# Pooled-query attention with a feed-forward block: the low parts of q and k by an accumulating DMA, and row maxima in units of 512 keys

## The chip, the cores and the metric

One core of one Trainium2 chip. The metric is the device time of one execution in microseconds, from the first to the last instruction and what the launch adds around it; several runs are taken and their median is used. The profile is of one execution.

## The reference

Attention over 8 batches x 8 heads, 1152 keys and head dimension 64, where each two neighbouring queries are averaged first, so there are 576 queries. Then a feed-forward block on the 4608 tokens.

```python
q_pool = q.reshape(B, H, S // 2, 2, D).mean(axis=3)
scores = scale * np.matmul(q_pool, k.transpose(0, 1, 3, 2))
scores = scores - np.max(scores, axis=-1, keepdims=True)
attn = np.exp(scores); attn = attn / (attn.sum(-1, keepdims=True) + 1e-9)
x = np.matmul(attn, v)            # -> (4608, 512)
h = x @ w_in                      # (512, 2048)
return (h - np.tanh(h)) @ w_out   # (2048, 512)
```

All is float32. The kernel gets that precision on TensorE from two reduced-precision (fp32r) parts: `hi`, the rounded value, and `lo`, value minus `hi`; a product is hi·hi + hi·lo + lo·hi.

## The kernel before

Two heads of a batch are a *pair*: 32 pairs, with head 0 in partitions 0 to 63 and head 1 in 64 to 127. For a pair, `raw` (128 x 1728 floats) holds the summed queries (576) and the keys (1152); `w.hi` (`kq_h` in the profile) and `w.lo` (`kq_l`) are its two parts.

Every engine's instructions are issued in the order in which the program names them (`InOrder`), so a place in the program is a place in that engine's queue. DMAs go through SyncE's queue (`sp`).

Each pair has two phases, and each has 18 places (`NS = 18`):

- the *scores phase*, places 0 to 17. Each place makes one tile of scores, 128 keys x 288 queries for both heads, with four pairs of matmuls (hi·hi, lo·hi, hi·lo, and a row that subtracts the maximum: `sel` x `m_row`). ScalarE takes the exponential into `p`; GpSimd adds three `p` at a time into `sum`.
- the *PV phase*, places 18 to 35: 72 matmuls `ps<-p,v` into two outputs that ScalarE copies to `o_s` (after places 26 and 35), then `sums` (24 matmuls `sum,ones`, copied to `s_s`).

All PSUM results of the attention stage, scores, maxima, outputs and sums alike, take turns in one ring of four buffers (`ring`, tile `ps`, 2 x 512 floats each).

The exponential needs each query's maximum beforehand. It is taken from hi·hi of the *next* pair during the scores phase of the current one: `max_part(pi, i)` multiplies 128 queries by 384 keys for both heads, and VectorE reduces 128 x 768 to 128 x 2 (`mx<-ps`). Four query tiles x three thirds of the keys make units 0 to 11, at places 1, 2, 4, 5, 7, 8, ... 16, 17. The last 64 queries of both heads form one tile (`q_last`) and two units (12, 13) that are done at the end of the pair before. `max_row` (place 17) reduces the parts to `nm`, transposes them (`tr`) and sends them through DRAM (`m_dram`) to `m_row`.

What else is put at places of pair `p` (NS = 18):

- NS: `query_sums` (VectorE, `raw<-q`) and `high` (ScalarE, `kq_h<-raw`, `q_last<-raw`) for pair p+2
- NS + 8: `low` for pair p+1, the subtraction on VectorE (`kq_l<-raw,kq_h`), after `o_s` of the first half
- NS + 12: `load` of raw and q for pair p+3; place 2: `load_v` for p+1
- the weights of the feed-forward block, in 16 blocks of six steps. A step is taken at places NS + 3, 6, 11 and 15 of pairs from 2 on, so the steps repeat over three pairs. First step: ScalarE's absolute value (`w_t<-w_raw`) and VectorE's `w_hl<-w_off`; second: three VectorE operations on `w_t`; third: `w_hl<-w_raw,w_t` and the next block's loads; fourth: `w_t<-w_hl`; fifth: `w_hl<-w_hl,w_t` and the stores to `wi_dram` or `wo_dram`; sixth: nothing. `w_hl` is one buffer, so the next block's first VectorE operation on it waits for that store.
- in the last four pairs, the first chunk of x for the feed-forward block (VectorE `x_r`, `x_l`; ScalarE `x_h`).

The feed-forward stage then runs over 9 chunks of 512 tokens x 16 blocks of hidden units.

Of the kernel before, what the change touches and what calls it, by code (L numbers as in the profile page):

```python
# [7 lines left out]
F32 = mybir.dt.float32  # L8
F32R = mybir.dt.float32r
I32 = mybir.dt.int32  # L10
U16 = mybir.dt.uint16
AF = mybir.ActivationFunctionType
ALU = mybir.AluOpType
AX = mybir.AxisListType
# [32 lines left out]
def attention_ffn_kernel(  # L47
# [16 lines left out]
    P = 128  # L64
    B, NP, _, _, SQ = q.shape
    S = k.shape[-1]
    D = P // 2
    KT = S // P
    KQ = SQ + S
    HQ = SQ // 2  # L70
    CH = S // 3
# [5 lines left out]
    pe, act, dve, pool, sp = (InOrder(tc, e) for e in (nc.tensor, nc.scalar, nc.vector, nc.gpsimd, nc.sync))  # L77
# [32 lines left out]
    class X:  # L110
# [25 lines left out]
        def high(self, c):  # L136
            act.activation(self.h[:, c], self.r[c], AF.Copy)

        def low(self, eng, c):
            eng.tensor_tensor(self.l[:, c], self.r[c], self.h[:, c].bitcast(F32), op=ALU.subtract)  # L140
# [14 lines left out]
    with ExitStack() as actx:  # L155
        new = lambda name, bufs, **kw: actx.enter_context(tc.tile_pool(name=name, bufs=bufs, **kw))
        st = new("st", 1)
        hip, lop = new("hi", 2), new("lo", 1)
        vp = new("vp", 2)
        ppool = new("pp", 2)  # L160
        sp_pool = new("sums", 1)
        op = new("op", 2)
# [17 lines left out]
        def rows(t, h):  # L180
            return t[h * D:h * D + D]

        def psum():
            return ring.tile([P, 2, 512], F32, name="ps")
# [10 lines left out]
        pairs = {}  # L195
# [15 lines left out]
        def high(pi, parts=1):  # L211
# [4 lines left out]
            for h in range(2):  # L216
                act.activation(rows(q_last[pi % 2], h)[:, h * D:h * D + D], rows(w.raw, h)[:, 4 * P:SQ], AF.Copy)

        def low(pi):
            w = pairs[pi]  # L220
            w.lo = lop.tile([P, KQ], F32R, name="kq_l")
            dve.tensor_tensor(w.lo, w.raw, w.hi.bitcast(F32), op=ALU.subtract)

        def load_v(pi):
            w = pairs[pi]
# [1 line left out]
            sp.dma_start(w.v, v[w.b, w.hp])  # L227


        order = [(t, c) for t in range(4) for c in range(3)] + [(4, 0), (4, 2)]  # L230

        def max_part(pi, i):

            w = pairs[pi]
            t, c = order[i]
            q0 = t * P
            ps = psum()
            if t < 4:
                for h in range(2):
                    pe.matmul(ps[:, h, 0:CH], rows(w.hi, h)[:, q0:q0 + P], rows(w.hi, h)[:, SQ + c * CH:SQ + (c + 1) * CH],  # L240
                              start=True, stop=True)
                dve.tensor_reduce(w.mx[:, t, c], ps[:, :, 0:CH], axis=AX.X, op=ALU.max)
            else:
                n = min(2, 3 - c)
                for a in range(n):
                    pe.matmul(ps[:, a, 0:CH], q_last[pi % 2], w.hi[:, SQ + (c + a) * CH:SQ + (c + a + 1) * CH],
                              start=True, stop=True)
                dve.tensor_reduce(w.mx[:, 4, c // 2, 0:n], ps[:, 0:n, 0:CH], axis=AX.X, op=ALU.max)
# [70 lines left out]
        class W:  # L319
# [17 lines left out]
            def steps(self, then):  # L337
# [23 lines left out]
                def low():  # L361
# [6 lines left out]
                    high,  # L368
                    lambda: ts(self.t, self.hl[:, 0], -0x800000, None, op0=ALU.bitwise_and),
                    low,  # L370
                    lambda: None,
                ]
# [21 lines left out]
        NS = 2 * KT  # L394

        def add(pi, place, f, *args):
            at.setdefault((pi, place), []).append(lambda: f(*args))

        for pi in range(1, n_pair):
            for i in range(12):  # L400
                add(pi - 1, i // 2 * 3 + 1 + i % 2, max_part, pi, i)
            if pi >= 2:
                for i in range(12, 14):
                    add(pi - 2, 2 * NS, max_part, pi, i)
            add(pi - 1, NS - 1, max_row, pi)
        for pi in range(n_pair):
            if pi >= 2:
                add(max(pi - 3, 0), NS + 12 if pi > 2 else 0, load, pi)
                add(pi - 2, NS, query_sums, pi)
                add(pi - 2, NS, high, pi)  # L410
            if pi >= 1:
                add(pi - 1, 2, load_v, pi)
                add(pi - 1, NS + 8, low, pi)
            if pi % NP == NP - 1 and pi < n_pair - 1:
                add(pi + 1, 10, fetch_sums, pi // NP)
                add(pi + 1, NS + 10, reciprocals, pi // NP)
# [26 lines left out]
        load_v(0)  # L443
        query_sums(0)
        high(0, 2)
        for i in range(9):
            max_part(0, i)
        max_row(0, 0, 3)
        low(0)
        for i in range(9, 14):  # L450
            max_part(0, i)
        max_row(0, 3, 4)
        query_sums(1)
        high(1)
        for i in range(12, 14):
            max_part(1, i)
        blocks[0].load()

# [4 lines left out]
        for pi in range(n_pair):  # L463
            w = pairs[pi]
            ps = [Half(), Half()]
# [101 lines left out]
    for ci in range(len(chunks)):  # L567
        c = Chunk()
# [8 lines left out]
        for f in range(NF):  # L577
            n = ci * NF + f
# [71 lines left out]
```

## Time and profile before

| | |
|---|---|
| median of 3 runs | 1634.74 us (1633.24 to 1636.42) |
| the profiled execution | 1633.7 us, its span 1631.9 us, granted clock 0.996 |
| busy: PE, VectorE, ScalarE, GpSimd | 97%, 78%, 58%, 68% |
| attention stage | scores of pair 0 at 26.75 us, PV of pair 31 at 813.86 us |
| subtraction `kq_l` | 32 x 2783 ns = 89.1 us of VectorE |
| exponentials | 576 x 653 ns on ScalarE |
| reductions `mx` 128 x 768 | 416 x 953 ns on VectorE |

How to read it: DVE is VectorE, ACT ScalarE, POOL GpSimd, SP SyncE, PEld TensorE's weight loads, and a q behind a name is that engine's queue. A row of the groups gives out<-in, the shape, the count, then busy us and the mean ns of one, then the idle time just before them and what ended it. A row in order of time gives start and length in us; in brackets is the idle time before it and its releaser. Several like instructions in a row are merged with their count. A matmul's time includes its way through the array, so successive ones overlap, and a PE that is 97% busy isn't at its peak: a step between starts (0.13 us for two 288-column matmuls on the two halves of the array) tells the rate.

### The profile page before, as it was taken

The numbers are of one execution on the slowest core, as the hardware profiler recorded it, in microseconds if no ns is written. First come the engines' busy times: TensorE is split into PE (matmuls) and PEld (weight loads), VectorE is DVE, ScalarE is ACT, GpSimd is POOL, SyncE is SP. The second block draws the span as 40 slices with busy tenths as digits, with TensorE's granted clock in tenths as the row PEclk, the third lists the DMA queues.
The fourth block names the chain that finished last, engine by engine and source line by source line (L and its number), as shares of the span: only waits on it lengthen the run. The fifth ranks groups of instructions, "written<-read, shape, count | busy, mean of one in ns | idle before, by whom it ended". The sixth has DMA issues, their size and how long they took to land.

```text
span 1631.9 us, 30673 instructions
## 1 busy us (share of the span) xinstructions
PE 1586.2 (97%) x12012; PEld 1228.4 (75%) x12012; DVE 1280.5 (78%) x1621; ACT 938.5 (58%) x1584; POOL 1113.3 (68%) x749
## 2 busy tenths in 40 slices
PE   5999999999999999999999999999999999999998
PEld 4777676776776776777768888888888888888886
DVE  6788888898889898969447777777777777777776
ACT  3565565565655656656535656555555656555554
POOL 3777786776767767778756666666757675666654
PEclk9999999999999999999999999999999999999999
DMA  4335444344453554333471101001010101020000
GB/s 169 107 119 197 167 150 182 133 183 162 155 214 135 200 182 160 131 123 100 152 310 34 65 7 48 31 7 65 13 65 14 65 14 65 13 65 10 30 1 26
DMA packets 79602, 166.15 MB, mean 102 GB/s; under 512 B 11874, under 2 KB 38498, under 8 KB 77410
## 3 DMA queue, kind: packets, MB, share of 16 engines
q1 hardware_dynamic: 79458, 164.20, 28.3%
q8 instruction: 94, 1.54, 0.4%
q14 instruction: 50, 0.41, 0.1%
HBM read 126.12 MB, written 38.04 MB: 101 GB/s over the span
## 4 chain that ended last, share of the span: by engine, by line
PE 83%; DVE 11%; DMA 2%; issue 2%; ACT 2%; POOL 0%; SPq 0%; POOLq 0%; DVEq 0%; ACTq 0%
PE ps L37 35%; PE ps_h L37 24%; PE ps_o L37 24%; DVE mx L37 3%; DVE w_t L37 3%; DVE kq_l L37 1%; DVE w_hl L37 1%; DMA wi_dram<-w_hl 1%; DVE raw L37 1%; ACT w_t L37 1%; DMA m_dram<-tr 0%; SPq L37 0%; DMA q<-in_q_dram 0%; ACT q_last L37 0%; POOL sum L37 0%
## 5 line engine op out<-in xcount | busy, mean ns | idle before, releaser
L37 DVE TENSOR_REDUCE mx<-ps 128x2 f32<-128x768 f32 x448 | 396.6, 924 | 86.9 <-PE ps L37 85.0
L37 POOL TENSOR_TENSOR sum<-p,p 128x576 f32<-128x576 f32 x192 | 300.6, 1566 | 196.7 <-ACT p L37 196.5
L37 ACT ACTIVATE p<-ps 128x576 f32<-128x576 f32 x576 | 353.2, 653 | 112.1 <-PE ps L37 93.7
L37 POOL TENSOR_SCALAR g_m<-g_u 128x512 uint8<-128x512 f32 (+1 forms) x145 | 250.6, 1728 | 197.6 <-ACT g_u L37 182.5
L37 POOL TENSOR_TENSOR sum<-sum,p 128x576 f32<-128x576 f32 x192 | 301.1, 1568 | 29.2 <-ACT p L37 15.1
L37 PE MATMUL ps<-kq_h 64*128 64x288 f32 (+1 forms) x1920 | 289.3, 345 | 28.0 <-DVE mx L37 17.6
L37 PE MATMUL ps<-p,v 128*64 128x288 f32 x2304 | 286.4, 407 | 0.1
L37 DVE SCALAR_TENSOR_TENSOR ps_w<-g_u,ps_h 128x512 f32<-128x512 f32 (+1 forms) x145 | 100.4, 693 | 191.3 <-ACT g_t L37 191.2
L37 PEld LDWEIGHTS ps<-p,v 128*64 128x64 f32 x2304 | 162.6, 137 | 114.4 <-ACT p L37 6.9
L37 POOL TENSOR_TENSOR g_lo<-g_s,g_hi 128x512 fp32r<-128x512 f32 (+1 forms) x145 | 186.6, 1287 | 89.5 <-ACT g_hi L37 89.5
L37 PE MATMUL ps_o<-w,g_hi 128*128 128x512 f32 x792 | 244.5, 390 | 1.0 <-ACT g_hi L37 1.0
L37 PEld LDWEIGHTS ps<-kq_h 64*128 64x128 f32 x1920 | 181.3, 187 | 80.8 <-DVE mx L37 33.0
L37 ACT ACTIVATE g_u<-ps_h 128x512 f32<-128x512 f32 (+1 forms) x145 | 85.8, 591 | 244.0 <-PE ps_h L37 242.3
L37 PE MATMUL ps_h<-x_h,w 128*128 128x512 f32 (+1 forms) x800 | 214.8, 390 | 0.0
L37 ACT ACTIVATE g_s<-g_u,pc 128x512 f32<-128x512 f32 x290 | 193.2, 714 | 11.3
L37 PEld LDWEIGHTS ps_h<-x_h,w 128*128 128x128 f32 x800 | 149.6, 188 | 32.4
L37 PEld LDWEIGHTS ps_o<-w,g_hi 128*128 128x128 f32 x792 | 148.5, 188 | 33.6 <-ACT g_hi L37 1.4
L37 PE MATMUL ps<-kq_l,kq_h 64*128 64x288 f32 x1152 | 171.8, 295 | 0.0
L37 PE MATMUL ps<-kq_h,kq_l 64*128 64x288 f32 x1152 | 171.5, 294 | 0.0
L37 PE MATMUL ps<-m_row,sel 64*128 64x288 f32 x1152 | 171.2, 293 | 0.0
L37 PE MATMUL ps_o<-w,g_lo 128*128 128x512 f32 x396 | 154.8, 391 | 0.6 <-POOL g_lo L37 0.5
L37 DVE COPY_PREDICATED g_s<-g_m,g_t 128x512 f32<-128x512 uint8 (+1 forms) x145 | 108.4, 748 | 15.0
(92 smaller groups left out, 2368.3 us busy)
## 6 DMA issues: line engine op xcount, KB each, us to landing
raw<-in_k_dram SPq DMA_DIRECT2D x32, 576.0 KB
q<-in_q_dram SPq DMA_DIRECT2D x32, 576.0 KB
v<-in_v_dram SPq DMA_DIRECT2D x32, 576.0 KB
x_dram<-o_s SPq DMA_DIRECT2D x32, 288.0 KB
x_l<-x_dram SPq DMA_DIRECT2D x9, 1024.0 KB
out_dram<-o_f SPq DMA_DIRECT2D x36, 256.0 KB
w_raw<-in_w_in_dram SPq DMA_DIRECT2D x8, 1024.0 KB
w_off<-in_w_in_dram SPq DMA_DIRECT2D x8, 1024.0 KB
```

Source lines behind the costliest of these rows:

```text
L37: i = f(*args, **kwargs)
```

## The change

1. `low` no longer subtracts on VectorE, except for pair 0. Instead ScalarE writes -raw, rounded to fp32r like `hi`, into the tile of `lo` (`minus_high`, place NS + 9 of the pair two before), and GpSimd issues a DMA that adds `raw` onto it (`low`, place NS + 16 of the pair two before). `lo` has two buffers instead of one.
2. The maxima of the four full query tiles (4 x 1152 keys) are taken in nine units of 512 keys instead of twelve of 384. A unit that crosses from one query tile to the next is in two pieces, each with its own matmuls and reduction: units 2, 4 and 6 (128 + 384, 256 + 256, 384 + 128). There are still three parts for each tile, 24 matmuls and 12 reductions. The units stand at places 1, 3, 5, ... 17.
3. In the prologue, seven units, then pair 0's subtraction, then the last two; and `minus_high` and `low` for pair 1 ahead of its two `q_last` units.

```diff
-        hip, lop = new("hi", 2), new("lo", 1)
+        hip, lop = new("hi", 2), new("lo", 2)
...
+        def minus_high(pi):
+            w = pairs[pi]
+            w.lo = lop.tile([P, KQ], F32R, name="kq_l")
+            act.activation(w.lo, w.raw, AF.Copy, scale=-1.0)
+
         def low(pi):
             w = pairs[pi]
-            w.lo = lop.tile([P, KQ], F32R, name="kq_l")
-            dve.tensor_tensor(w.lo, w.raw, w.hi.bitcast(F32), op=ALU.subtract)
+            if pi == 0:
+                w.lo = lop.tile([P, KQ], F32R, name="kq_l")
+                dve.tensor_tensor(w.lo, w.raw, w.hi.bitcast(F32), op=ALU.subtract)
+                return
+            pool.dma_start(w.lo.bitcast(F32), w.raw, accum_op=ALU.add, max_dma_last_dim=4 * KQ)
...
-        order = [(t, c) for t in range(4) for c in range(3)] + [(4, 0), (4, 2)]
+        units, n_part = [], {}
+        for u in range(0, 4 * S, 512):
+            units.append([])
+            left = 512
+            while left:
+                t, k0 = divmod(u, S)
+                n = min(S - k0, left)
+                units[-1].append((t, n_part.setdefault(t, 0), k0, n))
+                n_part[t] += 1
+                u, left = u + n, left - n
+        NU = len(units)
...
-            t, c = order[i]
-            q0 = t * P
             ps = psum()
-            if t < 4:
-                for h in range(2):
-                    pe.matmul(ps[:, h, 0:CH], rows(w.hi, h)[:, q0:q0 + P], rows(w.hi, h)[:, SQ + c * CH:SQ + (c + 1) * CH],
-                              start=True, stop=True)
-                dve.tensor_reduce(w.mx[:, t, c], ps[:, :, 0:CH], axis=AX.X, op=ALU.max)
+            if i < NU:
+                at_ = 0
+                for t, c, k0, n in units[i]:
+                    for h in range(2):
+                        pe.matmul(ps[:, h, at_:at_ + n], rows(w.hi, h)[:, t * P:(t + 1) * P], rows(w.hi, h)[:, SQ + k0:SQ + k0 + n],
+                                  start=True, stop=True)
+                    at_ += n
+                at_ = 0
+                for t, c, k0, n in units[i]:
+                    dve.tensor_reduce(w.mx[:, t, c], ps[:, :, at_:at_ + n], axis=AX.X, op=ALU.max)
+                    at_ += n
...
-            for i in range(12):
-                add(pi - 1, i // 2 * 3 + 1 + i % 2, max_part, pi, i)
+            for i in range(NU):
+                add(pi - 1, 2 * i + 1, max_part, pi, i)
...
+                add(pi - 2, NS + 9, minus_high, pi)
+                add(pi - 2, NS + 16, low, pi)
...
-                add(pi - 1, NS + 8, low, pi)
...
-        for i in range(9):
+        for i in range(7):
             max_part(0, i)
         max_row(0, 0, 3)
         low(0)
-        for i in range(9, 14):
+        for i in range(7, NU + 2):
             max_part(0, i)
...
         high(1)
-        for i in range(12, 14):
+        minus_high(1)
+        low(1)
+        for i in range(NU, NU + 2):
             max_part(1, i)
```

More of the change, by code (lines that the diff above doesn't have):

```diff
@@ L227, in load_v @@
             sp.dma_start(w.v, v[w.b, w.hp])
-        order = [(t, c) for t in range(4) for c in range(3)] + [(4, 0), (4, 2)]
+        units, n_part = [], {}
[8 more added lines that the diff above has]
+                u, left = u + n, left - n
+        assert set(n_part.values()) == {3}
+        NU = len(units)
         def max_part(pi, i):
             w = pairs[pi]
-            t, c = order[i]
-            q0 = t * P
             ps = psum()
-            if t < 4:
-                for h in range(2):
-                    pe.matmul(ps[:, h, 0:CH], rows(w.hi, h)[:, q0:q0 + P], rows(w.hi, h)[:, SQ + c * CH:SQ + (c + 1) * CH],
-                              start=True, stop=True)
-                dve.tensor_reduce(w.mx[:, t, c], ps[:, :, 0:CH], axis=AX.X, op=ALU.max)
+            if i < NU:
[9 more added lines that the diff above has]
+                    at_ += n
             else:
+                c = 2 * (i - NU)
                 n = min(2, 3 - c)
@@ L454, in attention_ffn_kernel @@
         high(1)
-        for i in range(12, 14):
+        minus_high(1)
+        low(1)
+        for i in range(NU, NU + 2):
             max_part(1, i)
```

## The prediction

> **What bounds the kernel now.** I read the page first (engines, chain), then the times at which one pair's PV products follow another's, then single pairs in order of time.
>
> ```profile
> span 1631.9 us, 30673 instructions
> PE 1586.2 (97%) x12012; PEld 1228.4 (75%) x12012; DVE 1280.5 (78%) x1621; ACT 938.5 (58%) x1584; POOL 1113.3 (68%) x749
> PE 83%; DVE 11%; DMA 2%; issue 2%; ACT 2%; POOL 0%; SPq 0%; POOLq 0%; DVEq 0%; ACTq 0%
> ```
>
> TensorE sets the time; VectorE holds 11% of the chain that ended last, and a gain has to come from there, in the attention stage. The next rows show the PV products of the first and the last of 32 pairs, then stretches from PV to PV (columns: length, then busy time of PE, weight loads, VectorE, ScalarE, GpSimd, then granted clock, DMA share, GB/s). The first sum is over the eight stretches of the kind 89.49:115.50, the second over the eight of the kind 115.50:140.47.
>
> ```profile
> 41.28 8.95 PE L37 MATMUL ps<-p,v 128*64 128x288 f32 x72
> ...
> 813.86 8.95 PE L37 MATMUL ps<-p,v 128*64 128x288 f32 x72
> ...
> 65.38:89.49 24.11, 24.11 (x270) 17.77 (x268) 17.05 (x20) 14.35 (x25) 18.95 (x13) 1.00 0.26 91
> 89.49:115.50 26.01, 24.45 (x269) 17.84 (x268) 22.64 (x26) 15.42 (x25) 18.20 (x13) 1.00 0.43 164
> 115.50:140.47 24.97, 24.61 (x269) 17.87 (x267) 21.69 (x25) 15.42 (x25) 20.25 (x14) 1.00 0.41 130
> 140.47:164.59 24.12, 24.12 (x270) 17.76 (x268) 22.17 (x25) 14.36 (x25) 17.40 (x13) 1.00 0.65 221
> ...
> 390.83:418.43 27.60, 25.94 (x270) 19.48 (x268) 23.01 (x27) 15.57 (x26) 19.49 (x14) 0.94 0.41 155
> sum 212.31, PE 198.65 PEld 145.96 DVE 182.48 ACT 123.59 POOL 147.66; mean PE 24.83 PEld 18.25 DVE 22.81 ACT 15.45 POOL 18.46
> sum 199.08, PE 195.60 PEld 142.65 DVE 178.68 ACT 123.91 POOL 152.78; mean PE 24.45 PEld 17.83 DVE 22.33 ACT 15.49 POOL 19.10
> ```
>
> An undisturbed pair takes 24.11. The weight blocks repeat over three pairs, which I call A, B and C in that order: 26.01, 24.97, 24.12. The 31 stretches take 813.86 - 41.28 = 772.58, and 31 x 24.11 is 747.4: 25.2 us of stalls. Eight A hold 212.31 - 8 x 24.11 = 19.4 of them, eight B 199.08 - 192.88 = 6.2. (Two late pairs with x work on VectorE lose about as much as the short last stretch saves.) In some A the stall also lowers the granted clock (0.94 at 390.83).
>
> An A pair in order of time; the last row is from the chain:
>
> ```profile
> 95.50 1.40 POOL L37 TENSOR_TENSOR sum<-sum,p 128x576 f32<-128x576 f32 x1
> 95.66 3.26 DVE L37 TENSOR_SCALAR w_t<-w_t 128x1024 f32<-128x1024 f32 x3 [1.51 <-ACT w_t L37]
> 98.48 0.41 ACT L37 ACTIVATE o_s<-ps 128x288 f32<-128x288 f32 x1 [2.57 <-PE ps L37]
> 98.83 1.95 DVE L37 TENSOR_TENSOR kq_l<-raw,kq_h 128x1728 fp32r<-128x1728 f32 x1
> 100.67 0.19 PEld L37 LDWEIGHTS ps<-kq_h 64*128 64x128 f32 x2 [0.25 <-ACT s_s L37]
> 100.70 1.22 DVE L37 SCALAR_TENSOR_TENSOR w_hl<-w_raw,w_t 128x1024 int32<-128x1024 int32 x1
> 101.95 0.70 DVE L37 TENSOR_SCALAR w_t<-w_hl 128x1024 int32<-128x1024 int32 x1
> 102.56 0.95 DVE L37 TENSOR_REDUCE mx<-ps 128x2 f32<-128x768 f32 x1
> 102.87 1.40 POOL L37 TENSOR_TENSOR sum<-p,p 128x576 f32<-128x576 f32 x1 [5.96 <-ACT p L37]
> ...
> 95.66 1.81 DVE w_t L37
> ```
>
> Scores begin at 100.67, but VectorE starts the first maximum only at 102.56, because kq_l, w_hl and w_t stand before it. Four PSUM buffers go round, so TensorE soon waits for that maximum. In an undisturbed pair (below) the first maximum starts at 226.49 with scores at 226.56, so here it is due at 100.60 and 1.96 late: the pair's 1.9 us.
>
> A B pair:
>
> ```profile
> 117.87 2.44 DVE L37 SCALAR_TENSOR_TENSOR w_hl<-w_hl,w_t 128x1024 fp32r<-128x1024 int32 x1
> 120.02 1.02 SPq L37 DMA_DIRECT2D wi_dram<-w_hl  x2
> 120.24 3.17 DVE L37 TENSOR_TENSOR kq_l<-raw,kq_h 128x1728 fp32r<-128x1728 f32 x1
> 123.44 0.34 SPq L37 DMA_DIRECT2D raw<-in_k_dram  x1
> 124.58 0.70 DVE L37 TENSOR_SCALAR w_hl<-w_off 128x1024 int32<-128x1024 int32 x1 [1.17 <-DMA wi_dram<-w_hl]
> 126.69 0.19 PEld L37 LDWEIGHTS ps<-kq_h 64*128 64x128 f32 x2 [0.24 <-ACT s_s L37]
> 127.25 0.95 DVE L37 TENSOR_REDUCE mx<-ps 128x2 f32<-128x768 f32 x1
> ...
> 120.51 3.95 DMA wi_dram<-w_hl
> ...
> L37 DVE TENSOR_SCALAR w_hl<-w_off 128x1024 int32<-128x1024 int32 x16 | 20.7, 1295 | 5.4 <-DMA wi_dram<-w_hl 3.3 <-DMA wo_dram<-w_hl 2.0
> ```
>
> Here kq_l lies in the 3.95 us in which w_hl is stored, and VectorE waits 1.17 more for that store.
>
> **The change part by part.**
>
> *kq_l off VectorE (31 of 32).* In undisturbed and C pairs it was hidden: nothing. In A it goes from the path: after the three w_t (95.66 + 3.26 = 98.92) come w_hl 1.22 and w_t 0.70, so the first maximum could start at about 100.7, against 100.60 due. The chain before it starts about 0.2 later (the last maximum of a pair is larger, next part), so it is 0.3 late. What is late next is the w_t after ScalarE's absolute value (1.51 wait). A new cost here: GpSimd issues the accumulating DMA after its last sum (95.50 + 1.40) and after ScalarE's new step (free at 98.48 - 2.57 = 95.91, plus 1.65), so from about 97.6, beside these VectorE operations. No row shows such an issue. Its price is from nothing to 1.1 per pair: the first w_t took 1.81 beside a GpSimd sum, against 0.70 without. I take 0.4, nearer nothing, since an issue carries no data through GpSimd. So A goes from 19.4 to 8 x 0.7 = 5.6: -13.8 us.
>
> The Trainium skill, page "SBUF — State Buffer", section "SBUF: two separate sides", says that VectorE and GpSimd share one port pair as an exclusive lock and that a GpSimd DMA cannot write its descriptors while VectorE holds it. The 1.81 against 0.70 agrees with the lock; its use for descriptors no run here shows.
>
> *B.* The store still ends the wait, so removing kq_l gives nothing where VectorE waited for it (5.4 us, of which 3.3 and 2.0 for the two stores). In the other B's kq_l ended after the landing, and up to 0.6 each may be won. Against that, 0.2 each for the later start, and raw's load, which SP held until kq_l was done (123.44), now goes out right behind the store. I take zero, between -3 and +5 us.
>
> *Nine units instead of twelve.* Rows of an undisturbed pair: the start of its scores phase, two maxima groups one cycle (three places) apart, and the groups of reductions by size.
>
> ```profile
> 226.49 1.42 DVE L37 TENSOR_REDUCE mx<-ps 128x2 f32<-128x768 f32 x2 [0.28 <-PE ps L37]
> 226.56 0.40 PE L37 MATMUL ps<-kq_h 64*128 64x288 f32 x2
> 226.79 0.30 PE L37 MATMUL ps<-kq_l,kq_h 64*128 64x288 f32 x2
> 226.92 0.29 PE L37 MATMUL ps<-kq_h,kq_l 64*128 64x288 f32 x2
> ...
> 232.38 1.82 DVE L37 TENSOR_REDUCE mx<-ps 128x2 f32<-128x768 f32 x2 [0.33 <-PE ps L37]
> 234.54 1.82 DVE L37 TENSOR_REDUCE mx<-ps 128x2 f32<-128x768 f32 x2 [0.35 <-PE ps L37]
> ...
> L37 DVE TENSOR_REDUCE mx<-ps 128x2 f32<-128x768 f32 x403 | 370.3, 953 | 85.4 <-PE ps L37 83.5
> ...
> L37 DVE TENSOR_REDUCE mx<-ps 128x1 f32<-128x384 f32 x31 | 16.9, 547 | 0.0
> ...
> L37 ACT ACTIVATE kq_h<-raw 128x1728 fp32r<-128x1728 f32 x31 | 51.0, 1646 | 81.2 <-DVE raw L37 81.2
> ```
>
> The work stays: 24 matmuls and 12 reductions per pair, the same columns. From 547 ns for 384 and 953 for 768 elements a reduction is about 0.14 + 1.06 ns per element: 1.23 for 1024, and about 1.29 for a unit in two pieces (less the overlap of two in a row). What changes is the ring of four buffers. The old phase is six cycles of 2.16 (232.38 to 234.54), 12.9 in all. The new order is scores, scores, maximum: the first scores of a unit reuse the buffer of the maximum two units before. That loop is: scores that had to wait 0.23 + 3 x 0.13 (226.56, 226.79, 226.92) = 0.62, the second scores 0.53, the 512-column matmul's end about 0.39 later (0.29 and the added columns), the reduction 1.23 to 1.29, release 0.1: about 2.9 for two units, so 4.5 x 2.9 = 13.05. That is 0.15 more per phase. Without the loop nine units would be 9 x (0.53 + 0.53 + 0.23) = 11.6, which bounds it below; a double unit of 3.2 would bound it above at 14.4. I take +0.15, the loop by rows, with -0.4 to +0.5 as likely ends. It holds in 29 of 31 phases; in the two with x work VectorE sets the pace by sums of work that stay. 29 x 0.15 = +4.4 us.
>
> *-hi on ScalarE.* One activation of kq_h's size, 1.65 us, 31 times. It stands in the PV phase behind the first o_s; behind it wait the second o_s, in B the absolute value of w_raw, then the next pair's exponentials. ScalarE idles 2.57 before that o_s in A, the fullest kind, so 0.9 is left: nothing. Without that cover it would be up to 1.65 a pair.
>
> *The DMA.* 31 times 0.88 MB within SBUF, queued on GpSimd behind the pair's sums. The 1 MB store landed in 3.95 us; at a third of that rate it would take 10, and kq_l is first read a whole pair (24 us) later: nothing. GpSimd idles 5.96 before the next sum (102.87), which covers the issue; each us beyond that would cost up to 31. By the fit of the skill's page "DMA: Bandwidth & Descriptors", section "Anatomy of one DMA", a plain copy of this size would be an estimated 4.0 us, and no run here shows it for an accumulating one.
>
> *SP queue.* The loads of raw no longer wait for kq_l (they wait for an accumulation of a pair earlier). *Prologue:* pair 0 keeps its subtraction and the reductions sum to the same; the extra ScalarE step falls beside the last maxima of pair 1. The feed-forward stage has none of the edits.
>
> Sum: -13.8 + 0 + 4.4 = -9.4. The profiled execution took 1633.7 (span 1631.9), 1.0 under the median of 1634.74: 1625.3 against the median.
>
> **The rivals.**
>
> *The ring costs more (slower).* The units wait for their own reductions longer than I reckon. For it: a unit's two pieces may be reduced only when both are done, and the loop has no slack at all. Against: VectorE idles 0.33 in each old cycle. It decides from 13.4 per phase on (13.8 / 29 = 0.48 more than now); at 13.8 it gives 29 x 0.9 - 13.8 = +12: 1647.
>
> *The ring gains.* The loop is softer than reckoned and phases approach 12.3: 29 x -0.6 - 13.8 = -31: 1604. For it: old cycles waited for exponentials, which the new order spaces out. Against: the reuse distance above.
>
> *The lock takes A's gain (no change).* The issue delays VectorE by 1.1 or more in each A: 0.3 + 1.1 = 1.4 late, 8.2 gained instead of 13.8, less 4.4: -4, and twice that delay +5: 1631 to 1640. For it: the 1.81 row. Against: by then most of A's chain has passed.
>
> *Hidden anyway.* B's and C's rows speak for it, but A's stall is plainly in the chain.
>
> **How the numbers follow.** My forecast 0.56, ring slower 0.16, ring faster 0.13, lock 0.15. The forecast's own ends are A 17 to 10, B -3 to +5, phases -9 to +10. A range from 1608 to 1641 reaches half into both ring rivals and leaves out 2 in 10. A measurement here tells about 0.2% (3.3 us) from no change. Faster: most of the forecast, the fast ring, some of the lock: 0.66. Same: the lock and the forecast's edge: 0.17. Slower: the slow ring: 0.17.
>
> **What would show it.** Right: no kq_l group on VectorE but one; A stretches of about 25 at granted clock 1.00, undisturbed ones of about 24.3; in the scores phase, weight loads waiting for mx rather than p; B still waiting for the store. Wrong: undisturbed stretches above 24.6 or below 23.8, w_t or w_hl in A above 1.81 beside the new DMA, sums on GpSimd starting later than 13.4 us after PV.

## The result and the profile after

The changed kernel takes 1649.85 us (median of 6 runs, 1646.92 to 1651.67) against 1633.99 (6 runs, 1631.49 to 1636.42): 1.0096 of the time before, 95% interval 1.0081 to 1.0111. It is slower by 1%, where 1625.3 was predicted. One of the ten runs of e4_one_reduce below took 1937.57 us at a granted clock of 0.755; the ratios leave it out.

The page of the changed kernel: span, engines, chain that ended last.

```profile
span 1646.0 us, 30912 instructions
PE 1588.0 (96%) x12012; PEld 1225.8 (74%) x12012; DVE 1212.8 (74%) x1590; ACT 977.8 (59%) x1615; POOL 1112.4 (68%) x780
...
PE 85%; DVE 9%; DMA 4%; issue 1%; ACT 1%; SPq 0%; POOLq 0%; POOL 0%; DVEq 0%; ACTq 0%
```

VectorE lost 68 us of work and two points of the chain, as it should. But the span grew by 14.1, and DMA went from 2% to 4% of the chain. Where it went shows in the stretches from one pair's PV products to the next (columns as before: length, busy PE, weight loads, VectorE, ScalarE, GpSimd, granted clock, DMA share, GB/s): one undisturbed, an A, two B, two of the late pairs with x work; then the sums over the eight A and the eight B.

```profile
66.47:91.21 24.74, 24.30 (x269) 17.66 (x268) 14.91 (x18) 15.68 (x27) 18.20 (x14) 1.00 0.43 123
91.21:115.93 24.72, 24.31 (x269) 17.70 (x267) 20.73 (x24) 16.60 (x28) 18.55 (x14) 1.00 0.60 190
115.93:142.44 26.51, 24.71 (x269) 17.73 (x268) 19.82 (x23) 16.70 (x28) 19.49 (x15) 1.00 0.61 174
...
191.92:220.89 28.97, 26.00 (x270) 19.24 (x268) 19.87 (x23) 17.03 (x28) 20.27 (x15) 0.94 0.56 159
...
749.35:778.93 29.58, 25.57 (x269) 19.16 (x267) 21.55 (x24) 16.68 (x29) 21.48 (x16) 0.94 0.46 123
778.93:810.66 31.73, 25.86 (x269) 19.43 (x268) 17.76 (x22) 16.89 (x29) 18.90 (x14) 0.89 0.57 183
...
sum 198.15, PE 195.00 PEld 141.68 DVE 166.30 ACT 133.05 POOL 148.76; mean PE 24.38 PEld 17.71 DVE 20.79 ACT 16.63 POOL 18.60
sum 212.70, PE 200.24 PEld 145.01 DVE 161.99 ACT 134.04 POOL 157.54; mean PE 25.03 PEld 18.13 DVE 20.25 ACT 16.76 POOL 19.69
```

Take the undisturbed stretch (24.73 now, 24.11 before) as the base of each kernel, and count what A, B and the three x stretches have above it: A 198.15 - 8 x 24.73 = 0.3, B 212.70 - 197.84 = 14.9 (14.8 with the base unrounded). The last, short stretch is 20.21 in both. The 14.1 us then divide so:

| part | before | after | difference |
|---|---|---|---|
| base of a stretch, x 30 | 24.11 | 24.73 | +18.7 |
| eight A above base | 19.5 | 0.3 | -19.2 |
| eight B above base | 6.2 | 14.8 | +8.6 |
| three x stretches above base | 3.4 | 11.8 | +8.4 |
| ahead of the first PV | 41.28 | 41.73 | +0.5 |
| after the last PV | 818.0 | 815.1 | -2.9 |

The last row is no part of the change. In both kernels TensorE waits 3.44 us for VectorE's `g_t` as the feed-forward stage begins (until 834.24 before, until 851.24 after). These are the 6.8 us around the end of that wait, first before, then after.

```profile
833.36:840.16 6.80, 5.92 (x14) 4.67 (x15) 5.56 (x9) 0.97 (x2) 1.28 (x1) 0.50 1.03 418
```

```profile
850.37:857.17 6.80, 5.93 (x25) 4.81 (x26) 5.85 (x10) 3.29 (x6) 2.78 (x2) 1.00 1.02 419
```

Before, it ran at half the clock; after, at full clock. Of the kernels below, some had such a slow stretch of 3.4 us there and some none, so these 3 us are read as chance.

The clock moves time between the other rows too. In these traces it is 1.00 or, for one to three periods of 3.41 us, 0.50. In the attention stage before, two such periods lie in A (from 406.70 and 481.79); after, two lie in B (207.85 and 436.54) and three in the x stretches (774.46, and two from 801.77). A period costs about 1.5 us: the two A stretches of before that have one take 27.60 and 27.37, four others 26.0. So an estimated 3 us each of what A gained, of what B lost and of what the x stretches lost is clock. The length of the wait does not settle which stretch gets one: before, TensorE waits 1.5 to 2.0 us in all eight A, and two of the 1.54 ones have it while the two longest (1.99) do not. So a part that differs by 1.5 between single profiles may differ by that alone.

**The gain in A, in order of time** (an A pair of the changed kernel; its scores begin at 102.40):

```profile
98.21 2.15 DVE L37 TENSOR_SCALAR w_t<-w_t 128x1024 f32<-128x1024 f32 x3 [1.50 <-ACT w_t L37]
100.30 0.89 POOL L37 DMA_DIRECT2D kq_l<-raw  x1 [2.30 <-PE ps L37]
100.39 1.23 DVE L37 SCALAR_TENSOR_TENSOR w_hl<-w_raw,w_t 128x1024 int32<-128x1024 int32 x1
101.66 0.69 DVE L37 TENSOR_SCALAR w_t<-w_hl 128x1024 int32<-128x1024 int32 x1
102.34 1.42 DVE L37 TENSOR_REDUCE mx<-ps 128x2 f32<-128x768 f32 x2
```

The first maximum starts at 102.34, before the scores at 102.40. It isn't late at all. The issue of the accumulating DMA on GpSimd (100.30 to 101.19) lies beside w_hl, and that takes 1.23 against 1.22 before; in the other seven A it lies there too, and w_hl takes 1.16 to 1.23. It costs VectorE nothing here. The three w_t even fell from 3.26 to 2.15, since GpSimd's sum had ended before them.

**The loss in the ring.** The reductions and the new work, by group (attention stage of the changed kernel: count, busy time, mean ns, idle time before and what ended it):

```profile
L37 DVE TENSOR_REDUCE mx<-ps 128x2 f32<-128x1024 f32 x186 | 227.8, 1225 | 37.1 <-PE ps L37 32.0
L37 DVE TENSOR_TENSOR raw<-q 128x576 f32<-128x576 f32 x30 | 48.7, 1623 | 0.1
L37 POOL DMA_DIRECT2D kq_l<-raw x31 | 27.3, 881 | 71.7 <-ACT kq_l L37 49.0 <-PE ps L37 18.4 <-DMA raw<-in_k_dram 3.5
L37 ACT ACTIVATE kq_l<-raw 128x1728 fp32r<-128x1728 f32 x31 | 50.9, 1643 | 0.5
L37 DVE TENSOR_SCALAR w_hl<-w_off 128x1024 int32<-128x1024 int32 x16 | 20.9, 1304 | 29.3 <-DMA wi_dram<-w_hl 18.0 <-DMA wo_dram<-w_hl 11.3
```

A whole unit's reduction takes 1225 ns, as worked out. 186 is six a pair; the other three units of each pair lie across two query tiles and are reduced in two pieces. What the weight loads of the scores waited for shows the difference (30 to 800 us; idle time, times, longest): first before, then after.

```profile
PEld ps L37 <- DVE mx L37: 28.4, 51, 2.2
PEld ps L37 <- ACT p L37: 28.0, 134, 1.4
```

```profile
PEld ps L37 <- PE ps L37: 38.1, 89, 0.5
PEld ps L37 <- DVE mx L37: 25.2, 68, 2.7
```

The exponentials no longer hold TensorE. In their place come 89 waits, three a pair, put down to TensorE's own products, which did not exist before. They stand at the scores that reuse the buffer of a split unit: there two semaphores are waited for. Ahead of each of the 89 loads the trace has a wait of its own for VectorE's semaphore (0.05 us), and the load itself waits for a count of TensorE's own.

**The loss in B** (a B pair of the changed kernel, PV at 191.92, and what its second half waited for):

```profile
193.79 1.80 DVE L37 TENSOR_TENSOR raw<-q 128x576 f32<-128x576 f32 x1
195.52 2.44 DVE L37 SCALAR_TENSOR_TENSOR w_hl<-w_hl,w_t 128x1024 fp32r<-128x1024 int32 x1
196.57 1.79 SPq L37 DMA_DIRECT2D wi_dram<-w_hl  x2
198.46 1.76 SPq L37 DMA_DIRECT2D raw<-in_k_dram  x1
200.08 0.88 POOL L37 DMA_DIRECT2D kq_l<-raw  x1 [0.85 <-ACT kq_l L37]
203.24 0.69 DVE L37 TENSOR_SCALAR w_hl<-w_off 128x1024 int32<-128x1024 int32 x1 [5.29 <-DMA wi_dram<-w_hl]
206.92 0.87 PE L37 MATMUL ps<-kq_h 64*128 64x512 f32 x4 [2.48 <-DVE mx L37]
```

VectorE has nothing to do from 197.95 on and waits 5.29 for the store; the wait of all 16 such steps grew from 5.4 to 29.3 us. TensorE then waits 2.48, and the granted clock is 0.50 for 3.41 us from 207.85 on, which makes 0.94 of the stretch. The load of raw goes out at 198.46, 6.5 after PV, right behind the store, where it stood 8.7 after PV before (mean).

### The profile page after: what moved, and what is told of

It reads as the page before. It is cut to its first block, busy times and chain, and to the rows that moved or that the text cites. A ratio compares the mean times of both kernels' runs of the same rounds, so it can differ in the third digit from the quotient of the medians.

```text
span 1646.0 us, 30912 instructions
## 1 busy us (share of the span) xinstructions
PE 1588.0 (96%) x12012; PEld 1225.8 (74%) x12012; DVE 1212.8 (74%) x1590; ACT 977.8 (59%) x1615; POOL 1112.4 (68%) x780
## 3 DMA queue, kind: packets, MB, share of 16 engines
q8 instruction: 94, 1.54, 0.4%
## 4 chain that ended last, share of the span: by engine, by line
PE 85%; DVE 9%; DMA 4%; issue 1%; ACT 1%; SPq 0%; POOLq 0%; POOL 0%; DVEq 0%; ACTq 0%
PE ps L37 37%; PE ps_h L37 24%; PE ps_o L37 24%; DVE mx L37 4%; DMA x_r<-r_dram 2%; DVE w_hl L37 1%; DMA wi_dram<-w_hl 1%; DVE raw L37 1%; DVE w_t L37 1%; DMA wo_dram<-w_hl 1%; SPq L37 0%; DMA q<-in_q_dram 0%; DVE x_r L37 0%; DVE ps_w L37 0%; ACT g_s L37 0%
## 5 line engine op out<-in xcount | busy, mean ns | idle before, releaser
L37 DVE TENSOR_REDUCE mx<-ps 128x2 f32<-128x1024 f32 (+3 forms) x448 | 403.4, 926 | 137.4 <-PE ps L37 132.1
L37 ACT ACTIVATE p<-ps 128x576 f32<-128x576 f32 x576 | 343.7, 652 | 127.8 <-PE ps L37 120.2
L37 POOL TENSOR_TENSOR sum<-p,p 128x576 f32<-128x576 f32 x192 | 287.1, 1496 | 144.8 <-ACT p L37 144.8
L37 POOL TENSOR_SCALAR g_m<-g_u 128x512 uint8<-128x512 f32 (+1 forms) x145 | 246.4, 1700 | 194.3 <-ACT g_u L37 179.2
L37 PE MATMUL ps<-kq_h 64*128 64x288 f32 (+4 forms) x1920 | 302.9, 342 | 39.9 <-DVE mx L37 25.9
L37 POOL TENSOR_TENSOR sum<-sum,p 128x576 f32<-128x576 f32 x192 | 290.4, 1513 | 23.2 <-ACT p L37 8.6
L37 PEld LDWEIGHTS ps<-kq_h 64*128 64x128 f32 x1920 | 187.4, 189 | 95.8 <-PE ps L37 40.0
L37 PE MATMUL ps<-kq_l,kq_h 64*128 64x288 f32 x1152 | 181.1, 296 | 0.0
L37 PE MATMUL ps<-kq_h,kq_l 64*128 64x288 f32 x1152 | 180.6, 295 | 0.0
L37 PE MATMUL ps<-m_row,sel 64*128 64x288 f32 x1152 | 180.2, 294 | 0.0
## 6 DMA issues: line engine op xcount, KB each, us to landing
kq_l<-raw POOLq DMA_DIRECT2D x31, 864.0 KB, 10.6
```

What stands on the lines that cost most here:

```text
L37: i = f(*args, **kwargs)
```

## The experiments

What each has above its own base in us, from one profiled execution each, its median time (four to ten runs, e9 two), and its ratio to the kernel before on the same chip:

| kernel | base | A | B | x | median us | ratio to before (95%) |
|---|---|---|---|---|---|---|
| before | 24.11 | 19.5 | 6.2 | 3.4 | 1633.99 | |
| after | 24.73 | 0.3 | 14.8 | 11.8 | 1649.85 | 1.0096 (1.0081 to 1.0111) |
| e1_lo_only | 24.11 | 2.6 | 11.7 | 9.1 | 1626.92 | 0.9950 (0.9931 to 0.9969) |
| e2_max_only | 24.73 | 14.9 | 10.8 | 2.3 | 1653.95 | 1.0126 (1.0101 to 1.0152) |
| e3_no_dma | 24.73 | 0.2 | 14.6 | 2.3 | 1641.06 | 1.0036 (1.0020 to 1.0051) |
| e4_one_reduce | 24.29 | 0.7 | 11.8 | 11.4 | 1634.13 | 0.9995 (0.9981 to 1.0009) |
| e5_load_late | 24.10 | 2.9 | 7.8 | 8.6 | 1622.15 | 0.9919 (0.9894 to 0.9945) |
| e6_load_late_last_dve | 24.11 | 2.8 | 6.4 | 3.3 | 1616.48 | 0.9892 (0.9870 to 0.9915) |
| e8_nine_mended | 24.73 | 0.3 | 15.6 | 2.3 | 1640.43 | 1.0048 (1.0033 to 1.0062) |
| e9_two_reduces | 24.89 | 0.1 | 11.4 | 8.6 | 1648.39 | 1.0094 (1.0074 to 1.0114) |

**One half at a time.** e1_lo_only is the kernel before with the new lo alone; e2_max_only is the changed kernel with the old subtraction.

```
 e1: before, and
-                add(pi - 1, NS + 8, low, pi)
+                add(pi - 2, NS + 9, minus_high, pi)
+                add(pi - 2, NS + 16, low, pi)        # accumulating DMA; lo in two buffers
 e2: after, with these lines the other way round
```

> The low parts by ScalarE and the accumulating DMA, with the twelve old units of 384 keys. Theory R (the nine units cost 0.63 us in each scores phase, some 19 in all; the DMA costs what B and x pairs lost, 17): undisturbed stretches from PV to PV back to 24.11, A stretches without a stall (about 24.1), B and x pairs as late as in the changed kernel; 1628 to 1636 us. Theory D (the accumulating DMA slows everything, the units are innocent): undisturbed stretches stay near 24.7 and the time above 1643.

> Nine units of 512 keys, with the old subtraction on VectorE. Theory R: undisturbed stretches 24.73, A and B stalls as before or 0.2 longer, x pairs as before: 1634 + 19 = 1651 to 1656 us. Theory D: 1633 to 1638.

Undisturbed stretch, A stretch and sum of B of e1:

```profile
65.69:89.81 24.12, 24.12 (x269) 17.75 (x268) 13.95 (x19) 16.00 (x26) 18.10 (x14) 1.00 0.44 127
89.81:114.10 24.29, 24.26 (x269) 17.83 (x267) 20.91 (x25) 16.93 (x26) 19.18 (x14) 1.00 0.61 190
...
sum 204.53, PE 196.81 PEld 144.15 DVE 154.15 ACT 136.53 POOL 154.69; mean PE 24.60 PEld 18.02 DVE 19.27 ACT 17.07 POOL 19.34
```

The same two stretches of e2:

```profile
66.87:91.60 24.73, 24.30 (x270) 17.69 (x268) 18.03 (x19) 14.02 (x26) 18.96 (x13) 1.00 0.26 88
91.60:117.90 26.30, 24.70 (x269) 17.77 (x267) 22.45 (x25) 15.08 (x27) 18.14 (x14) 1.00 0.44 163
```

In the base the halves separate cleanly. The nine units alone raise the base to 24.73; the new lo alone leaves it at 24.11 and takes A away. The lo half makes the kernel faster by 0.5% and the unit half makes it slower by 1.3%. B grows in both halves, and the x stretches with the new lo alone. Two forecasts missed: e1 came out 1 us below the 1628 to 1636 of theory R, and e2 has A at 14.9 and B at 10.8, where A and B as before (19.5 and 6.2) were expected; together they are 25.7 in both.

**The DMA's traffic.** e3_no_dma is the changed kernel without the accumulating DMA, so the adding of raw is left out.

```
-            pool.dma_start(w.lo.bitcast(F32), w.raw, accum_op=ALU.add, max_dma_last_dim=4 * KQ)
```

> The changed kernel with the accumulating DMA left out (lo stays at minus hi, so the adding is not done). Theory R: undisturbed stretches still 24.73; B's excess falls from 14.9 to 6 or less and that of the x pairs from 11.9 to about 3.4, if DMA traffic is what made them late: 1631 to 1637. Rival S (the loads of raw that now follow the store at once, not the accumulating DMA, made them late): B and x pairs stay as in the changed kernel, 1645 to 1650.

A late pair of e3 with x work, and its sum of B:

```profile
775.24:801.10 25.86, 24.29 (x269) 17.65 (x267) 19.35 (x22) 16.58 (x29) 18.51 (x13) 1.00 0.52 190
...
sum 212.49, PE 200.22 PEld 145.13 DVE 162.21 ACT 134.18 POOL 150.33; mean PE 25.03 PEld 18.14 DVE 20.28 ACT 16.77 POOL 18.79
```

The x stretches fell from 11.8 to 2.3: there the traffic was the cause. In the changed kernel VectorE waited for the fetch of x_r:

```profile
DVE x_r L37 <- DMA x_r<-r_dram: 7.7, 2, 5.4
```

B stayed at 14.6, so in B the traffic of this DMA is not the cause, and theory R was wrong there. The time of 1641.06 lies between both forecasts, as the x stretches followed one and B the other.

**The split units.** e4_one_reduce is the changed kernel with one reduction for each unit, over four parts of 128 keys at once, none of which crosses a tile; e9_two_reduces does the same in two halves, for every unit.

```
 e4: after, and
-                for t, c, k0, n in units[i]:
-                    dve.tensor_reduce(w.mx[:, t, c], ps[:, :, at_:at_ + n], axis=AX.X, op=ALU.max)
+                dve.tensor_reduce(w.mx[:, 4*i:4*i + 4], ps.rearrange("p h (a n) -> p a h n", n=P), axis=AX.X, op=ALU.max)
 e9: e4, and
+                for a in range(0, 4, 2):    # halves a:a + 2 of the same unit
```

> The changed kernel with one reduction per unit (four parts of 128 keys written at once; nine reductions instead of twelve). Theory W (a unit in two pieces makes the next user of its buffer wait on two semaphores, 0.1 us each time, three times a pair, and its second reduction adds 0.06): undisturbed stretches 24.3 to 24.5, time 1638 to 1644. Rival L (the ring's loop alone makes the 0.63): stretches 24.65 or more, time 1647 to 1651.

> As e4, but every unit of 512 keys, whole or in two pieces, is reduced in two instructions of half the width. Theory W (a second reduction on a buffer makes its next user wait on two semaphores, 0.1 us, and adds 0.06 of its own): the loop of two units grows by 0.16, four times a phase, so undisturbed stretches of 24.8 to 25.0 against 24.29. Rival P (the pieces of the matmul make the second wait, in three units only): 24.5.

An undisturbed stretch of e4, then its weight loads' waits, then its reductions:

```profile
66.00:90.28 24.28, 24.28 (x269) 17.66 (x267) 14.92 (x15) 15.67 (x27) 18.19 (x14) 1.00 0.45 127
```

```profile
PEld ps L37 <- DVE mx L37: 47.4, 151, 8.5
```

```profile
L37 DVE TENSOR_REDUCE mx<-ps 128x8 f32<-128x1024 f32 x279 | 341.4, 1225 | 64.7 <-PE ps L37 57.5
```

An undisturbed stretch of e9, then its weight loads' waits:

```profile
68.04:92.94 24.90, 24.47 (x269) 17.81 (x267) 15.10 (x24) 15.66 (x27) 18.22 (x14) 1.00 0.44 123
```

```profile
PEld ps L37 <- PE ps L37: 53.3, 152, 0.6
```

With the same products in the same ring, one reduction a unit takes the base from 24.73 to 24.29 and the waits for TensorE's own count are gone; two for every unit take it to 24.89, and there are 152 of them, five a pair. The fifth is at the first PV product and costs nothing: the load idles 0.27 there in both. Per wait that holds scores it is 0.44 / 3 = 0.15 and 0.60 / 4 = 0.15 us. So the second piece of a reduction is the cause of 0.44 of the 0.62; that a unit's matmuls come in two pieces is not, since they do so in e4 as well. The records divide the 0.15: a unit in two pieces ends 0.06 later, the weight load starts 0.12 after the end of the last piece instead of 0.05, and the first product starts 0.03 after its load instead of at once (medians over the 89 waits, and over those for VectorE in e4). This division is only read, since no run changed the one without the other. The 0.18 that stays is near the 0.15 predicted for the ring: the scores phase of e4 is 13.09 (77.19 to 90.28), and 13.05 was reckoned. The time of e4, 1634.13, is that of the kernel before, and below the 1638 to 1644 that theory W gave: nine units without pieces still take back what lo gains.

**When the loads go out.** e5_load_late is e1 with the loads of raw and q five places later in the pair; e6_load_late_last_dve has besides the last two pairs' lo from VectorE, without the DMA.

```
 e5: e1, and
-                add(max(pi - 3, 0), NS + 12 if pi > 2 else 0, load, pi)
+                add(max(pi - 3, 0), NS + 17 if pi > 2 else 0, load, pi)
 e6: e5, and
+        BY_DVE = (0, n_pair - 2, n_pair - 1)     # lo by the old subtraction, in the old place
```

> As e1 (old units, low parts by the accumulating DMA), with the loads of raw and q for pair p+3 issued at place NS + 17 instead of NS + 12, so some 3 us later and not right behind the store of w_hl. Theory S (B is late because the loads, no longer held back by kq_l, share the DMA engines with the store): the eight B lose 3 to 6 us in all instead of 11.7, the wait of w_hl for its store falls from 34 us to below 22; 1619 to 1624 us. Rival K (the accumulating DMA or VectorE's own order makes B late): B stays at 11 or more, 1625 to 1629.

> As e5, and the low parts of the last two pairs (30 and 31) by the old subtraction on VectorE, so no accumulating DMA runs beside the fetches of x_r. Theory X (those two accumulations make x_r late): the three x stretches lose 3 to 4 us in all instead of 9.1; 5 to 6 us less than e5: 1613 to 1618. Rival (x_r is late through the weight loads of the feed-forward stage): the same as e5.

Sum of B of e5:

```profile
sum 200.66, PE 196.72 PEld 144.10 DVE 155.48 ACT 136.69 POOL 154.88; mean PE 24.59 PEld 18.01 DVE 19.43 ACT 17.09 POOL 19.36
```

A late x stretch of e6 and its sum of B:

```profile
752.52:778.28 25.76, 24.58 (x270) 17.78 (x268) 22.62 (x24) 15.52 (x27) 18.58 (x13) 1.00 0.53 191
...
sum 199.22, PE 195.35 PEld 142.50 DVE 155.40 ACT 136.54 POOL 154.34; mean PE 24.42 PEld 17.81 DVE 19.42 ACT 17.07 POOL 19.29
```

B fell from 11.7 to 7.8 in e5 and to 6.4 in e6, where it is 6.2 before: with twelve units most of B's rise came from loads that went out beside the store. The mean time from the start of the store's last issue to its landing went from 4.24 to 3.55 us. Of the 1.4 from e5 to e6, more than all lies in one stretch (27.44 and 25.79), which has a half-clock period in e5 and none in e6. Theory S was met in the time, but not in two numbers: B was to be 3 to 6, and VectorE's wait for the store fell from 34 to 29 us only (below 22 was expected). So B was won back while most of the wait stayed; much of that wait is time in which nothing else was due. The ratios of e1 and e5 alone have intervals that overlap (0.9931 to 0.9969 and 0.9894 to 0.9945); those of e1 and e6 do not. With the last two pairs on VectorE the x stretches are at 3.3, as before. e6 is the best version of all: 1616.48 (1615.55 to 1620.52), 1.1% under the kernel before and 2% under the changed one.

**The same mending with nine units.** e8_nine_mended is the changed kernel with the two edits of e5 and e6.

> The changed kernel with the loads of raw and q at place NS + 17 and the last two pairs' low parts by subtraction on VectorE, the nine units kept. If the loads and the last two accumulations are what it lost outside the ring: undisturbed stretches still 24.73, x stretches lose 2 to 3 us instead of 11.8, B 8 to 11 instead of 14.8; 1634 to 1638 us, so no better than before. Rival (the changed kernel has a further cost): 1642 or more.

An undisturbed stretch, the worst B and the sum of B:

```profile
66.73:91.47 24.74, 24.33 (x270) 17.71 (x268) 14.93 (x18) 15.67 (x27) 18.23 (x14) 1.00 0.44 125
...
417.16:447.34 30.18, 25.85 (x269) 19.13 (x267) 20.95 (x23) 16.81 (x28) 19.77 (x15) 0.94 0.52 158
...
sum 213.43, PE 199.95 PEld 144.85 DVE 163.72 ACT 134.07 POOL 156.05; mean PE 24.99 PEld 18.11 DVE 20.46 ACT 16.76 POOL 19.51
```

The x stretches fell to 2.3, as expected, but B stayed at 15.6, where 8 to 11 was expected. The time, 1640.43, is above the 1634 to 1638 expected, and under the 1642 of the rival. So here B has another cause than with twelve units. Three of its stretches (27.29, 30.18, 29.94) hold 13.2 of the 15.6, the others 0.2 to 0.8 each.

What the traces show of these, without a run that tests it: from the start of its last issue the store lands after 5.0 to 5.4 us in these three stretches of e8 and 2.8 to 3.2 in the others; in the changed kernel after 4.6 to 5.1 in the three longest (28.97, 28.21, 26.82) and 3.0 to 4.2 in the others. In each of the six a 16 KB packet of the instruction queue, 0.9 to 1.8 us long, runs on one of the 16 DMA engines about as the store begins, and in none of the others. It is so in e2 and e3 (three stretches each) and in e9 (one) as well: of the 40 B stretches of these five kernels, the 13 with such a packet (it starts between 0.3 us ahead of the store's last issue and 1.4 behind) are the 13 whose store landed latest, 4.5 to 5.4 us against at most 4.2. In the other five kernels, e4 among them with nine units in one reduction each, no B has a packet that starts in that span. The queues of the changed kernel in 196.9 to 199.4, within the B pair shown above:

```profile
q1 hardware_dynamic: 1210, 0.60, 80.3%
q8 instruction: 1, 0.02, 2.2%
```

One packet takes 2.2% of 16 engines x 2.5 us, 0.9 us of one engine. The store is besides issued 0.6 later than before (its issue ends 6.4 against 5.8 us after PV, means), and ahead of it raw<-q takes 1.62 us on VectorE in place of 1.07. That hangs on who starts first: where a GpSimd sum is already under way, raw<-q ends 0.6 after that sum (193.79 to 195.59, the sum ending at 194.98); in the kernel before, at 117.23, raw<-q began just ahead of the sum and took 0.72, and the sum took 1.99 instead of 1.40. But the delay is the same in all eight B of the changed kernel (last issue 5.9 to 6.1 after PV), so it does not tell the late ones from the others, and the packet does. Whether the packet makes them late, alone or only with the delay, stays open.

## Why the prediction was wrong

- **A, predicted -13.8, measured -19.2.** The mechanism was right: kq_l goes from VectorE's path and the first maximum is on time. The 0.3 of lateness and the 0.4 for the issue on GpSimd did not come; about 3 of the 19.2 are the two half-clock periods that A had before and has no more. The rival of the lock had no part in it: w_hl beside the issue kept its time. That the rule of the Trainium skill's page "SBUF — State Buffer", section "SBUF: two separate sides", holds for descriptors is thus not seen here; in the pair shown no VectorE step beside the issue was longer, nor was the issue (0.89, mean 0.88).
- **Nine units, predicted +4.4, measured +18.7.** This is the first step that failed, by the size of one term. The loop of two units takes 2.89 without a split unit (e4, 83.00 to 85.89), as the 2.9 of the prediction, but 3.04 with one (86.64 to 89.68 in the changed kernel): the scores phase went to 13.54, not 13.05. The sum had the second piece's own time (1.29 for 1.23), but not the second semaphore for which the next weight load then waits, some 0.09. The second pieces make 13 of the 18.7, as e4 shows. The rival "the ring costs more" named both the pieces and the missing slack, put its turning point at 13.4 and its time at 1647 for 13.8; it is what happened in kind. That 1647 is near the 1649.85 is luck: its ring is 13.8, not 13.54, and it has nothing for B and the x stretches.
- **B, predicted zero within -3 to +5, measured +8.6.** The prediction saw that raw's load would go out right behind the store, and gave it no price. With twelve units B rose by 5.5, and moving the loads gave 3.9 of it back (5.3 in e6). The changed kernel has a second cause, not settled above; about 3 of its 8.6 are two half-clock periods.
- **x pairs, predicted nothing, measured +8.4.** "VectorE sets the pace by sums of work that stay" overlooked a transfer: x_r is fetched while the accumulating DMA runs, and VectorE waits up to 5.4 us for it; three half-clock periods come with these waits. Taking the DMA away from these pairs (e3, e6, e8) took the cost away each time.
- **The DMA, predicted nothing.** Right for its own landing, which the bound of 10 us came close to, and for the issue on GpSimd; wrong for its neighbours, as the x pairs show.
- **ScalarE, predicted nothing: right.** The activation took 1643 ns, 1.65 was reckoned, and the base of e1 is unchanged at 24.11.
- **The profile's signs.** "Undisturbed stretches above 24.6" had been named as what would show it wrong, and they are 24.73. A came as foretold. The waits for p went, as foretold too, but the larger part of what took their place is put down to TensorE's own count and not to mx.

With the measured terms the prediction's own sum gives -19.2 + 8.6 + 18.7 + 8.4 = +16.5, which the head (+0.5) and the tail (-2.9) make 14.1. With the ring at the predicted +4.4 it would have been about no change (+2.2 ahead of head and tail); with B and x at nothing as well, a gain of 15. e6, which keeps twelve units and has B and x as before, gained 18.6 (1635.06, the kernel before on its chip, less 1616.48).

## What to carry to other kernels

In a ring of buffers without slack, count the instructions that free a buffer, not only their elements: a second reduction cost 0.15 us each time that TensorE waited for its buffer, and three a pair cost 13 us. When a step is taken off the engine that issues or holds back others, ask which transfers it had kept apart: here two of them, raw's loads and the DMA itself, ran into a store and a fetch for which an engine waited. A change of two halves is worth trying in halves: one half was a gain here and the other a loss larger than it. And where single profiles are set against each other part by part, look at the granted clock of each part first.

## What the runs showed of the hardware

The accumulating DMA (changed kernel: its row among the DMA issues, with KB and median us to landing, and its queue's packets, MB and share of 16 engines):

```profile
q0 software_dynamic: 4464, 27.43, 8.6%
...
kq_l<-raw POOLq DMA_DIRECT2D x31, 864.0 KB, 10.6
```

It landed 10.6 us after its issue in the median (6.3 to 13.1), in packets of 6.9 KB, and GpSimd took 0.88 us to issue it. The plain-copy estimate of 4.0 that the prediction gave by the Trainium skill's page "DMA: Bandwidth & Descriptors", section "Anatomy of one DMA", is far below; the bound from the store's rate (10) was near. The granted clock can fall after short waits: after the 2.48 us of the B pair shown, and after two of the six waits of 1.53 or 1.54 us in the A stretches before, it was 0.50 for 3.41 us.
